# A four-layer attention kernel on one core: single V buffers, 64-row input and output groups, 77 resident weight pieces, first rows copied by VectorE and a new issue list

## The chip, the core and the metric

The kernel runs on one core of one Trainium2 chip. The metric is device time in microseconds (us), lower is better. Each time below is the median of several executions. The runs came in four sets, each on one chip with the kernel before beside it; since the kernel before takes 3261 to 3275 us in different sets, kernels of different sets are compared by their ratios to it.

## The reference

Two layers, A and B, are applied in the order A, B, A, B to x, 2048 rows of 640, each as x + layer(layernorm(x)). Layer A works through segments of 32 rows, one after the other, because each hands 8 memory rows to the next:

```python
for s in range(n_seg):                       # 64 segments
    h = concatenate([mem, xs], axis=1)       # 8 memory rows + 32 rows
    q, k, v = h @ Wq, h @ Wk, h @ Wv         # 32 heads of 192
    p = softmax(where(mask, q k^T * scale, -1e9))
    o = (p v) @ Wo
    mem = o[:, :M, :]                        # to the next segment
    outs.append(o[:, M:, :])
# layer B: 32 heads of 20; each row sees itself and 7 earlier rows, 2 apart; then @ wo
```

The weights of A are 31.5 MB in bf16 and do not all fit into the core's memory.

## The kernel before

The two A layers are run as two *lanes* of one step: lane 0 is segment t of the first A, lane 1 is segment t-2 of the second, so one weight load serves 80 columns. There are 66 steps with layer A; steps 0 and 1 and steps 64 and 65 have one lane, the 62 between have both. Layer B of the step before is woven into each step, and a 67th step holds B alone.

The weights of A are 128 pieces of 224 or 256 KB. `N_RES` of them stay in memory; the rest are loaded again in every step, through a ring of 8 buffers, as TensorE frees them.

```python
RING = 8
N_RES = 74
...
    def load_piece(self, u):
        ...
        if res:
            t_ = self.wres.tile([P, w], BF16, name="w_{}{}_{}{}".format(*u))
        else:
            t_ = self.wring.tile([P, P * PIECE[0]], BF16, name="w_ring")
        ...
        self.nc.sync.dma_start(out=t_[:, 0:w], in_=src)
```

Each step issues its parts in the order of a fixed list. `K3`, `Q3`, `V3` are projections of the third quad of heads (30 matmuls each), `KE3`, `QE3`, `VE3` their evictions from PSUM, `S` the scores, `T`/`TE` the transposes of V and their copy, `PO` the product with V, `R` the reciprocals of the softmax sums, `OT` the normalised outputs, `Oa`/`Ob` halves of the output projection. Names with small letters belong to layer B: `bo` transposes its outputs, `boE` evicts them, `by` is its output projection. The program gives every engine its own instructions in this order.

```python
ORDER = """
K0 V0 K0y KE0 Q0 QE0 VE0 K1 bst bmv KE1 Q1 S0 T0 E0 ...
... PO6 Oa3 T7 bo TE7 Ob3 R6 boE S7 OT16 E7 by OT26 ... X1 BSQ
""".split()
...
    def x_load(self, g):                       # 128 rows, one buffer
        self.xt[g] = self.xp.tile([P, NC, P], BF16, name="XT4")
        self.nc.scalar.dma_start(out=..., in_=self.x[g])
    def x_take(self, t):
        o = SEG * (t % 4)
        self.nc.gpsimd.tensor_copy(out=self.xin[t % 2][:, :, 0:SEG], in_=self.xt[t // 4][:, :, o:o + SEG])
...
            if n == "QE0":                     # in step t, nt = t + 1
                ...
                if nt % 4 == 3 and nt + 1 < self.n_seg:
                    self.x_load((nt + 1) // 4)
        if t == 0:
            self.load_b_weights()
```

Of the kernel before, what the change touches and what calls it, by code (L numbers as in the profile page):

```python
# [13 lines left out]
ALU = mybir.AluOpType  # L14
# [25 lines left out]
N_RES = 74  # L40
# [4 lines left out]
K0 V0 K0y KE0 Q0 QE0 VE0 K1 bst bmv KE1 Q1 S0 T0 E0 QE1 EM0 TE0 V1 br bap VE1 S1 K2 E1 Q2 T1 TE1 PO0 QE2 V2  # L45
KE2 R0 EM1 VE2 V3 bq S2 OT10 VE3 bqE E2 T2 OT20 T3 PO1 TE2 TE3 K3 R1 bk qx1 bkE qx0 KE3 OT11 V4 Q3 VE4 bs3
OT21 EM2 bs1 be3 PO2 QE3 bv be1 bs0 bvE Q4 be0 S3 Oa0 K4 eb0 qx2 R2 bs2 Oa1 QE4 OT12 E3 EM3 bs5 KE4 Q5 OT22
be2 S4 be5 QE5 PO3 Ob0 E4 T4 R3 K5 V5 EM4 KE5 bs4 VE5 eb5 eb2 TE4 OT13 V6 be4 OT23 eb3 eb1 VE6 S5 PO4 T5 Ob1
E5 Oa2 TE5 EM5 bt eb4 K6 btE R4 OT14 Q6 KE6 OT24 QE6 bp1 T6 PO5 on1 Ob2 R5 TE6 S6 E6 K7 V7 KE7 bp0 OT15 OT25
EM6 on0 Q7 QE7 VE7 PO6 Oa3 T7 bo TE7 Ob3 R6 boE S7 OT16 E7 by OT26 EM7 Oa5 byE LSQ PO7 Oa4 lst LMV R7 Ob4 Oa6  # L50
OT17 Ob5 OT27 Ob6 O7x LR O7y LAP O7z MEMa MEMb X1 BSQ
# [52 lines left out]
class Kernel:  # L104
    def __init__(self, ctx, tc, xT, m0T, wA, wqkv, wo, out):
# [7 lines left out]
        self.n_seg = 4 * xT.shape[0]  # L113
# [13 lines left out]
        self.n_big = self.n_ot = 0  # L127
        self.build_consts()

    def build_consts(self):  # L130
# [9 lines left out]
        def pers(name, shape, n, dt=BF16, zero=True):  # L140
            ts = []
            for j in range(n):
                t_ = cp.tile(shape, dt, name=f"{name}{j}")
                if zero:
                    nc.vector.memset(t_[:], 0.0)
                ts.append(t_)
            return ts
# [3 lines left out]
        self.m0T = pers("m0T", [P, NC, NM], 1, zero=False)[0]  # L151
        self.KF = pers("KF", [P, 4 * NT + 48], 2)
        self.Kz = pers("Kz", [P, 4 * NT + 48], 2)
        self.Vt = pers("Vt", [P, 1024], 2)
        for vt in self.Vt:
            for c in (192, 320, 704, 832):
                nc.vector.memset(vt[:, c:c + 64], 1.0)
        self.VT = pers("VT", [P, 6 * NT + 48], 2)
        self.x1 = pers("x1", [P, NC, NX], 1)[0]
        self.h2T = pers("h2T", [P, NC, NX], 1)[0]  # L160
        self.KB = pers("KB", [P, NBC, P], 1)[0]
        self.VB = pers("VB", [P, BH // 2, 2 * BD + 2], 1)[0]
        self.VTB = pers("VTB", [P, NC, P], 1)[0]
        nc.vector.memset(self.VB[:, :, BD:BD + 1], 1.0)
        self.On = pers("On", [P, 3 * P], 1)[0]
        self.eb = pers("EB", [P, BH // 2, 2, NX], 1, zero=False)[0]
        self.YT = pers("YT", [P, NC, P], 1, zero=False)[0]
        self.wqkv = cp.tile([P, NC, 3 * D], BF16, name="wqkv_sb")
# [47 lines left out]
        self.hmask = hm  # L216

    def load_b_weights(self):
        nc = self.nc
        nc.sync.dma_start(out=self.wqkv[:].rearrange("p c n -> p (c n)"), in_=self.b_src[0])  # L220
        nc.sync.dma_start(out=self.wo[:].rearrange("p m n -> p (m n)"), in_=self.b_src[1])
# [83 lines left out]
    def vE(self, i):  # L305
        vt = self.VT[i % 2][:, 0:6 * NT].rearrange("p (a n) -> p a n", a=6)
        self.nc.scalar.copy(out=vt[:, :, self.cs], in_=self.vp[i][:, 0:6 * NT].rearrange("p (a n) -> p a n", a=6)[:, :, self.cs])  # L307

    def a_t(self, i):
        nc = self.nc  # L310
        ps = self.big("ps_vt", (P, 6, P), BF16)
        for n in range(6):
            nc.tensor.transpose(out=ps[:, n, :], in_=self.VT[i % 2][:, NT * n:NT * n + P], identity=self.ident[:])  # L313
        self.tp[i] = ps

    def tE(self, i):
        nc = self.nc
        src = self.tp[i][0:NT].rearrange("p n e -> p (n e)").rearrange("p (a e) -> p a e", a=2)
        dst = self.Vt[i % 2][0:NT].rearrange("p (a e) -> p a e", a=2)
# [39 lines left out]
    def a_pv(self, i):  # L359
        nc = self.nc  # L360
        em = self.em[i]
        vt = self.Vt[i % 2]
# [8 lines left out]
    def ot1(self, i):  # L371
        self.n_ot += 1
        cs = self.cs
        ot = self.ap1.tile([P, 2, 3, NT], BF16, name="OT", tag=f"OT{self.n_ot % 3}")
# [95 lines left out]
    def b_proj(self, b, col0, name):  # L470
# [3 lines left out]
        for n in range(NBC):  # L474
            for c in range(NC):
                e0 = col0 + BHC * BD * n
# [335 lines left out]
```

## Time and profile before

| | before |
|---|---|
| median time | 3258.68 us (6 runs, 3249.38 to 3263.43) |
| TensorE busy | 96% |
| first weight matmul | 22.7 us |
| step 1 begins, step 2 begins | 97.4 us, 152.5 us |
| a two-lane step, mean of steps 4 to 62 | 48.30 us |
| step 64 begins; from there to the last matmul | 3147.1 us; 107.8 us |

A step begins at its first matmul of `K0`; these times are read from the trace. From the page, the engines (busy us, share of the span, instructions) and the DMA queues (packets, MB, share of 16 engines):

```profile
PE 3136.6 (96%) x85668; PEld 3083.6 (95%) x85668; DVE 2039.3 (63%) x6890; ACT 1993.5 (61%) x5215; POOL 40.8 (1%) x150
...
q1 hardware_dynamic: 524160, 901.84, 85.9%
q8 instruction: 671, 10.99, 1.3%
```

TensorE bounds the kernel. Queue q1 carries the weights; its packets took 86% of the time of the 16 DMA engines. Queue q8 brings TensorE's own instructions: 671 packets of 16 KiB, one for every 256 instructions.

The view by stretches, over 2700 us of the middle (busy us and number of instructions by engine, clock, DMA share, GB/s). A two-lane step has 1298 matmuls, so the count of matmuls in a fixed stretch is the rate: 2700 x 1298 / 72509 = 48.33 us a step.

```profile
core 0: us, PE busy (x) PEld busy (x) DVE busy (x) ACT busy (x) POOL busy (x), PEclk, DMA share, GB/s
300.00:3000.00 2700.00, 2662.75 (x72509) 2628.81 (x72506) 1739.79 (x5807) 1715.38 (x4419) 20.19 (x55) 1.00 0.88 282
```

30 matmuls of 80 columns take 1.08 us, 36 ns each. This agrees with columns / 2.4 GHz + 2.5 ns, which the Trainium skill states ("TensorE: Matmul & The Clock Gate", section Wait — 56ns, not 53.3ns?). Adding up a step's matmuls at such a pace gives 47.18 us. The missing 1.1 us are short gaps. The view of waits over the same stretch (engine, tile, line, releaser: us in all, times, longest):

```profile
PE ps_q L267 <- issue: 6.8, 14, 1.2
PE ps_k L267 <- issue: 5.5, 10, 1.0
PE ps_v L267 <- issue: 4.9, 8, 1.1
PE ps_s L335 <- issue: 2.9, 6, 0.7
...
PEld L594 <- issue: 10.7, 51, 0.5
```

The last line is one steady gap, 51 times in some 56 steps: the output projection of layer B (line 594) waits for `boE` on ScalarE. The others have no releaser, and their places change from step to step. One of them in the timeline (start, us, instruction, idle time before it):

```profile
642.63 0.38 PE L267 MATMUL ps_k<-hT_88,w_k_10_683 128*128 128x80 bf16 x6
643.99 0.23 PE L267 MATMUL ps_k<-hT_88,w_k_10_683 128*128 128x80 bf16 x2 [0.97 <-issue]
```

It stands within one resident piece, so it waits for no weight. In the trace, a packet of q8 had landed 1.58 us before 643.99 us, when the matmuls resumed. Besides the steady one at line 594, steps 4 to 62 hold 82 gaps over 0.15 us; 76 of them end 0.9 to 1.8 us after such a landing, three quarters 1.3 to 1.6 us after it. I call these 76 *fetch gaps*. Their size below is the excess of a start-to-start time over the matmul's pace, where it is over 0.15 us and ends 0.9 to 1.8 us after a landing, over steps 4 to 62. Before it is 0.75 us a step, and the gap at line 594 is 0.26 us.

A count in the trace shows what these gaps are. If all of TensorE's instructions (weight loads, matmuls, semaphore instructions) are numbered in order, 73 of the 76 stand in the same stretch of seven instructions of a block of 256; I call that place the *border*. A block with such a gap I call *late*; steps 4 to 62 hold 600 blocks. A border passes every 4.6 us. The next packet starts after it (1.53 us in the median), and TensorE resumes about 1.35 us after a late landing, so a packet that lands within some 3.2 us of the border (4.6 less 1.35, an estimate) should be in time for the next one. The trace bears it out: of 490 packets that landed within 3.2 us none left a late block, of 110 that landed later 73 did.

The start, in the timeline:

```profile
19.13 0.32 POOL L615 COPY xin_84<-XT_353 128x160 bf16<-128x160 bf16 x1
19.50 0.43 PE L429 MATMUL ps_st<-xin_84,ones 128*128 128x64 bf16 x5 [19.50 <-POOL xin_84 L615]
...
22.68 0.43 PE L267 MATMUL ps_k<-hT_88,w_k_00_387 128*128 128x40 bf16 x8 [2.39 <-DVE hT_88 L455]
```

GpSimd copies the first rows only after 18 us of building masks. And the largest wait of step 1, from the view of waits between 97 and 156 us:

```profile
PE ps_k L267 <- DMA w_ring<-in_wA_dram: 7.7, 1, 7.7
```

The ring's pieces stand behind the 3.28 MB of layer B's weights.

### The profile page before, as it was taken

The page shows a single profiled execution, that of the slowest core. Times are in us where ns is not written, and L with a number is a line of the kernel's source. Part 1 is how long each engine was busy: PE and PEld are TensorE (multiplying, and loading weights), DVE is VectorE, ACT ScalarE, POOL GpSimd, SP SyncE. Part 2 cuts the span into 40 slices and gives each one's busy share as a digit, 9 for nine tenths or more (in the row PEclk, how much of TensorE's full clock was granted, in tenths as well). Part 3 has the DMA queues.
Part 4 walks back from the last instruction along what each step waited for, and adds up shares of the span by engine and source line. Part 5 has one row for each costly group of instructions (what it writes and reads, how often), then busy time and mean ns, then how long its engine had stood idle before and what let it go on. Part 6 is the DMA issues. An engine that isn't in the chain of part 4 may idle for free.

```text
span 3258.3 us, 192948 instructions
## 1 busy us (share of the span) xinstructions
PE 3136.6 (96%) x85668; PEld 3083.6 (95%) x85668; DVE 2039.3 (63%) x6890; ACT 1993.5 (61%) x5215; POOL 40.8 (1%) x150
## 2 busy tenths in 40 slices
PE   5799999999999999999999999999999999999997
PEld 4799999999999999999999999999999999999996
DVE  2466666666666666666666666666666666666665
ACT  2366666566666666666666666666666666666654
POOL 2000000000000000000000000000000000000000
PEclk7799999999999999999999999999999999999999
DMA  9988988888888888888888888888888888888886
GB/s 325 324 279 279 291 277 284 282 277 283 279 281 284 281 283 281 280 280 282 278 289 277 275 291 276 283 287 279 284 279 279 288 280 288 277 282 279 286 286 215
DMA packets 529747, 919.44 MB, mean 282 GB/s; under 512 B 58896, under 2 KB 279184, under 8 KB 528784
## 3 DMA queue, kind: packets, MB, share of 16 engines
q1 hardware_dynamic: 524160, 901.84, 85.9%
q8 instruction: 671, 10.99, 1.3%
q10 hardware_dynamic: 4752, 5.26, 0.5%
q14 instruction: 164, 1.34, 0.1%
HBM read 904.24 MB, written 2.62 MB: 278 GB/s over the span
## 4 chain that ended last, share of the span: by engine, by line
PE 91%; ACT 3%; DMA 3%; issue 2%; POOL 0%; DVE 0%; ACTq 0%; POOLq 0%; SPq 0%
PE ps_k L267 17%; PE ps_v L267 17%; PE ps_q L267 17%; PE ps_vt L313 5%; PE ps_o L367 5%; PE ps_s L335 2%; PE ps_s L334 2%; PE ps_bq L477 2%; PE ps_by L594 2%; PE ps_bk L477 2%; PE ps_bs L530 2%; DMA w_ring<-in_wA_dram 2%; ACT R L354 2%; PE ps_bv L495 1%; PE ps_st L429 1%
## 5 line engine op out<-in xcount | busy, mean ns | idle before, releaser
L267 PEld LDWEIGHTS <-w_ring 128*128 128x128 bf16 x19866 | 881.1, 100 | 40.9 <-DMA w_ring<-in_wA_dram 19.7
L354 ACT ACTIVATE R<-ps_o 64x320 f32<-64x320 f32 (+1 forms) x1056 | 449.2, 425 | 357.1 <-PE ps_o L367 238.8
L302 DVE CAST QT<-ps_q 128x480 bf16<-128x480 f32 (+1 forms) x528 | 337.9, 640 | 426.9 <-PE ps_q L267 426.7
L296 ACT CAST KF_93<-ps_k 128x320 bf16<-128x320 f32 (+1 forms) x264 | 110.4, 418 | 424.5 <-PE ps_k L267 424.4
L387 PEld LDWEIGHTS <-w_ring 128*128 128x128 bf16 x6996 | 310.4, 100 | 13.1 <-issue 6.2
L322 DVE COPY Vt_103<-ps_vt 80x128 bf16<-80x128 bf16 x528 | 91.9, 213 | 307.4 <-PE ps_vt L313 307.0
L341 ACT ACTIVATE Em<-ps_s 80x320 bf16<-80x320 f32 (+1 forms) x528 | 224.8, 426 | 95.7 <-PE ps_s L335 92.0
L375 DVE TENSOR_TENSOR OT<-ps_o,R 128x320 bf16<-128x320 f32 (+1 forms) x528 | 251.8, 477 | 39.8 <-ACT R L356 18.1
L356 ACT ACTIVATE R<-R 128x320 f32<-128x320 f32 (+1 forms) x528 | 244.0, 462 | 16.8
L267 PE MATMUL ps_v<-hT_88,w_ring 128*128 128x80 bf16 (+1 forms) x3993 | 230.0, 201 | 5.2 <-DMA w_ring<-in_wA_dram 3.1
L267 PE MATMUL ps_v<-hT_90,w_ring 128*128 128x80 bf16 (+1 forms) x3993 | 228.8, 201 | 5.4 <-issue 4.7
L307 ACT CAST VT_115<-ps_v 128x480 bf16<-128x480 f32 (+1 forms) x264 | 144.4, 547 | 78.6 <-PE ps_v L267 78.1
L542 ACT ACTIVATE EB_130<-ps_bs 128x384 bf16<-128x384 f32 (+2 forms) x462 | 170.6, 415 | 33.7 <-PE ps_bs L530 32.1
L267 PE MATMUL ps_k<-hT_90,w_ring 128*128 128x80 bf16 (+1 forms) x3036 | 173.6, 201 | 12.2 <-DMA w_ring<-in_wA_dram 9.3
L347 DVE TENSOR_TENSOR Em<-Em,maskA 80x320 bf16<-80x320 bf16 (+1 forms) x528 | 165.2, 313 | 20.0 <-ACT Em L341 1.6
L267 PE MATMUL ps_k<-hT_88,w_ring 128*128 128x80 bf16 (+1 forms) x3036 | 173.5, 201 | 1.7 <-DMA w_ring<-in_wA_dram 1.2
L267 PE MATMUL ps_q<-hT_88,w_ring 128*128 128x80 bf16 (+1 forms) x2904 | 169.1, 201 | 3.3 <-issue 1.7
L381 DVE TENSOR_TENSOR OT<-ps_o,R 64x160 bf16<-64x160 f32 (+1 forms) x528 | 164.9, 312 | 7.2
L267 PE MATMUL ps_q<-hT_90,w_ring 128*128 128x80 bf16 (+1 forms) x2904 | 168.0, 201 | 0.0
L307 ACT CAST VT_113<-ps_v 128x480 bf16<-128x480 f32 (+1 forms) x264 | 144.4, 547 | 34.9 <-PE ps_v L267 29.6
L296 ACT CAST KF_95<-ps_k 128x320 bf16<-128x320 f32 (+1 forms) x264 | 110.7, 419 | 78.7 <-PE ps_k L267 77.9
L380 DVE TENSOR_TENSOR OT<-ps_o,R 64x160 bf16<-64x160 f32 (+1 forms) x528 | 158.5, 300 | 0.0
(3045 smaller groups left out, 8864.5 us busy)
## 6 DMA issues: line engine op xcount, KB each, us to landing
w_ring<-in_wA_dram SPq DMA_DIRECT2D x1914, 256.0 KB, 4.3
w_ring<-in_wA_dram SPq DMA_DIRECT2D x1650, 224.0 KB, 4.0
out_dram<-YT_131 ACTq DMA_DIRECT2D x16, 160.0 KB, 5.0
wqkv_sb<-in_wqkv_dram SPq DMA_DIRECT2D x1, 2400.0 KB, 10.1
wo_sb<-in_wo_dram SPq DMA_DIRECT2D x1, 800.0 KB, 11.5
w_k_00_387<-in_wA_dram SPq DMA_DIRECT2D x1, 256.0 KB, 3.0
w_k_10_406<-in_wA_dram SPq DMA_DIRECT2D x1, 256.0 KB, 3.9
w_v_10_439<-in_wA_dram SPq DMA_DIRECT2D x1, 256.0 KB, 4.3
```

Of the source, the lines that this page charges most:

```text
L267: self.nc.tensor.matmul(ps[:, NT * n + c0:NT * n + c1], lhsT=self.block(kind, i, h, k), rhs=hT[:, NT * c + c0:NT * c + c1], start=(h == 0 ...
L296: nc.scalar.copy(out=kf[:, :, :, cs], in_=pv[:, :, 0:3:2, cs])
L302: self.nc.vector.tensor_copy(out=qt[:, :, self.cs], in_=self.qp[i][:, 0:6 * NT].rearrange("p (a n) -> p a n", a=6)[:, :, self.cs])
L307: self.nc.scalar.copy(out=vt[:, :, self.cs], in_=self.vp[i][:, 0:6 * NT].rearrange("p (a n) -> p a n", a=6)[:, :, self.cs])
L341: self.nc.scalar.activation(out=e[0:NT, :, cs], in_=self.sv[i][0:NT, :, cs], func=ACT.Exp, scale=float(DH) ** -0.5)
L347: self.nc.vector.tensor_tensor(out=em[0:NT, :, cs], in0=em[0:NT, :, cs], in1=self.maskA[0:NT, cs].unsqueeze(1).to_broadcast([NT, 4, w]), o ...
L354: self.nc.scalar.activation(out=r[rows, :, :, self.cs], in_=d, func=ACT.Ln)
L356: self.nc.scalar.activation(out=rf, in_=rf, func=ACT.Exp, scale=-1.0)
L375: self.nc.vector.tensor_tensor(out=ot[:, :, 0:3:2, cs], in0=self.ov[:, :, 0:4:3, cs], in1=self.r[i][:, :, :, cs], op=ALU.mult)
L381: nc.vector.tensor_tensor(out=ot[64:P, :, 1, cs], in0=ov[0:64, :, 2, cs], in1=r[0:64, :, 1, cs], op=ALU.mult)
L387: self.nc.tensor.matmul(self.acc[c // 3][:, o:o + self.cs.stop - self.cs.start], lhsT=self.block("o", i, h, k), rhs=ot[:, m, self.cs], sta ...
L542: self.nc.scalar.activation(out=self.eb[:, h:h + n, a, :], in_=self.bsp[c][:, NX * o:NX * (o + n)].rearrange("p (h n) -> p h n", h=n), fun ...
```

## The change

Its intent is to free memory (one V buffer instead of two, input and output in groups of 64 rows), to use it for three more resident pieces and a fourth buffer for inputs of the output projection, to start sooner, to load layer B's weights in four parts during step 1, and to arrange the issue list so that the single buffers cost nothing. The core of the diff:

```diff
-N_RES = 74
+N_RES = 77
 ORDER = """
-K0 V0 K0y KE0 Q0 QE0 VE0 K1 bst bmv KE1 Q1 S0 T0 E0 QE1 EM0 TE0 V1 br bap VE1 S1 K2 E1 Q2 T1 TE1 PO0 QE2 V2
... (7 lines)
+K0 Q0 K0y V0 KE0 Q1 QE0 S0 VE0 K1 QE1 E0 bst KE1 T0 V1 EM0 TE0 bmv Q2 VE1 PO0 br S1 QE2 bap R0 K2 T1 E1 V2 KE2
... (4 lines)
+bs5 eb3 be5 Oa1 S6 PO5 eb5 VE6 E6 Ob1 eb4 bt eb1 T6 EM6 btE R5 V7 TE6 OT15 OT25 bp0 bp1 K7 on0 VE7 PO6 Q7 T7
+KE7 on1 Oa2 bo Ob2 R6 QE7 TE7 S7 boE by OT16 E7 OT26 Oa5 EM7 byE Oa3 PO7 Oa4 LSQ lst Ob3 Oa6 Ob4 R7 LMV OT17
... (1 line)
+LAST = """ ...                      # the list for the step that holds layer B alone
-        self.Vt = pers("Vt", [P, 1024], 2)
-        self.VT = pers("VT", [P, 6 * NT + 48], 2)
+        self.Vt = pers("Vt", [P, 1024], 1)[0]
+        self.VT = pers("VT", [P, 6 * NT + 48], 1)[0]
-        ot = self.ap1.tile([P, 2, 3, NT], BF16, name="OT", tag=f"OT{self.n_ot % 3}")
+        ot = self.ap1.tile([P, 2, 3, NT], BF16, name="OT", tag=f"OT{i % 4}")
...
+    def first_rows(self):                    # called before most buffers are cleared
...
+        nc.vector.tensor_copy(out=self.xin[0][:, :, 0:SEG], in_=self.xt[0][:, :, 0:SEG])
+        for n in ("LSQ", "lst", "LMV", "LR", "LAP"):
+            self.l_piece(n, 0)
...
-        self.xt[g] = self.xp.tile([P, NC, P], BF16, name="XT4")
+        self.xt[g] = self.xp.tile([P, NC, NX], BF16, name="XT2")
...
+            if t == 1 and n in ("bst", "bap", "bqE", "bvE"):
+                self.load_b_weights(("bst", "bap", "bqE", "bvE").index(n))
...
-                if nt % 4 == 3 and nt + 1 < self.n_seg:
-                    self.x_load((nt + 1) // 4)
-        if t == 0:
-            self.load_b_weights()
+                if nt % 2 == 1 and nt + 1 < self.n_seg:
+                    self.x_load((nt + 1) // 2)
```

Left out: the clearing of layer B's buffers moves from VectorE to GpSimd, layer B's weights are laid out in three parts, and the last group of heads has its own mask.

More of the change, by code (lines that the diff above doesn't have):

```diff
@@ L44 @@
 ORDER = """
-K0 V0 K0y KE0 Q0 QE0 VE0 K1 bst bmv KE1 Q1 S0 T0 E0 QE1 EM0 TE0 V1 br bap VE1 S1 K2 E1 Q2 T1 TE1 PO0 QE2 V2
-KE2 R0 EM1 VE2 V3 bq S2 OT10 VE3 bqE E2 T2 OT20 T3 PO1 TE2 TE3 K3 R1 bk qx1 bkE qx0 KE3 OT11 V4 Q3 VE4 bs3
-OT21 EM2 bs1 be3 PO2 QE3 bv be1 bs0 bvE Q4 be0 S3 Oa0 K4 eb0 qx2 R2 bs2 Oa1 QE4 OT12 E3 EM3 bs5 KE4 Q5 OT22
-be2 S4 be5 QE5 PO3 Ob0 E4 T4 R3 K5 V5 EM4 KE5 bs4 VE5 eb5 eb2 TE4 OT13 V6 be4 OT23 eb3 eb1 VE6 S5 PO4 T5 Ob1
-E5 Oa2 TE5 EM5 bt eb4 K6 btE R4 OT14 Q6 KE6 OT24 QE6 bp1 T6 PO5 on1 Ob2 R5 TE6 S6 E6 K7 V7 KE7 bp0 OT15 OT25
-EM6 on0 Q7 QE7 VE7 PO6 Oa3 T7 bo TE7 Ob3 R6 boE S7 OT16 E7 by OT26 EM7 Oa5 byE LSQ PO7 Oa4 lst LMV R7 Ob4 Oa6
-OT17 Ob5 OT27 Ob6 O7x LR O7y LAP O7z MEMa MEMb X1 BSQ
+K0 Q0 K0y V0 KE0 Q1 QE0 S0 VE0 K1 QE1 E0 bst KE1 T0 V1 EM0 TE0 bmv Q2 VE1 PO0 br S1 QE2 bap R0 K2 T1 E1 V2 KE2
+TE1 EM1 VE2 bq OT10 Q3 OT20 bqE S2 PO1 E2 QE3 T2 R1 V3 K3 VE3 TE2 KE3 V4 qx0 T3 OT11 bk OT21 EM2 VE4 PO2 TE3
+S3 bkE E3 Q4 bs0 K4 EM3 R2 be0 QE4 bs1 K5 OT12 Q5 be1 OT22 KE4 PO3 T4 KE5 qx2 qx1 S4 R3 Oa0 E4 QE5 V5 bs2 TE4
+OT13 VE5 EM4 K6 be2 S5 Q6 OT23 eb0 KE6 QE6 PO4 T5 bs3 Ob0 TE5 eb2 E5 bv EM5 R4 bs4 be3 OT14 V6 be4 OT24 bvE
+bs5 eb3 be5 Oa1 S6 PO5 eb5 VE6 E6 Ob1 eb4 bt eb1 T6 EM6 btE R5 V7 TE6 OT15 OT25 bp0 bp1 K7 on0 VE7 PO6 Q7 T7
+KE7 on1 Oa2 bo Ob2 R6 QE7 TE7 S7 boE by OT16 E7 OT26 Oa5 EM7 byE Oa3 PO7 Oa4 LSQ lst Ob3 Oa6 Ob4 R7 LMV OT17
+Ob6 Ob5 OT27 O7x O7y LR LAP O7z MEMa MEMb X1 BSQ
+""".split()
+LAST = """
+bst bmv br bap bq bqE bk qx0 bkE qx1 bs0 be0 bs1 be1 qx2 bv bs2 be2 eb0 bs3 be3 eb1 bvE bs4 be4 eb2 bs5 be5 eb3
+bt eb4 btE eb5 bp0 on0 bp1 on1 bo boE by byE
 """.split()
@@ L112, in __init__ @@
         self.out = out
-        self.n_seg = 4 * xT.shape[0]
+        self.n_seg = 2 * xT.shape[0]
         pool = lambda name, bufs, **kw: ctx.enter_context(tc.tile_pool(name=name, bufs=bufs, **kw))
@@ L126, in __init__ @@
         self.cur = {}
-        self.n_big = self.n_ot = 0
+        self.n_big = 0
+        self.xt, self.ots, self.qxs, self.kp, self.qp, self.vp, self.tp = {}, {}, {}, {}, {}, {}, {}
+        self.x_load(0)
         self.build_consts()
@@ L138, in build_consts, with pers @@
         self.ones = ones
-        def pers(name, shape, n, dt=BF16, zero=True):
+        def pers(name, shape, n, dt=BF16, zero=True, eng=nc.vector):
             ts = []
@@ L144, in pers @@
                 if zero:
-                    nc.vector.memset(t_[:], 0.0)
+                    eng.memset(t_[:], 0.0)
                 ts.append(t_)
@@ L151, in build_consts @@
         self.m0T = pers("m0T", [P, NC, NM], 1, zero=False)[0]
+        self.first_rows()
         self.KF = pers("KF", [P, 4 * NT + 48], 2)
         self.Kz = pers("Kz", [P, 4 * NT + 48], 2)
-        self.Vt = pers("Vt", [P, 1024], 2)
-        for vt in self.Vt:
-            for c in (192, 320, 704, 832):
-                nc.vector.memset(vt[:, c:c + 64], 1.0)
-        self.VT = pers("VT", [P, 6 * NT + 48], 2)
-        self.x1 = pers("x1", [P, NC, NX], 1)[0]
-        self.h2T = pers("h2T", [P, NC, NX], 1)[0]
-        self.KB = pers("KB", [P, NBC, P], 1)[0]
-        self.VB = pers("VB", [P, BH // 2, 2 * BD + 2], 1)[0]
-        self.VTB = pers("VTB", [P, NC, P], 1)[0]
-        nc.vector.memset(self.VB[:, :, BD:BD + 1], 1.0)
-        self.On = pers("On", [P, 3 * P], 1)[0]
+        self.Vt = pers("Vt", [P, 1024], 1)[0]
+        for c in (192, 320, 704, 832):
+            nc.vector.memset(self.Vt[:, c:c + 64], 1.0)
+        self.VT = pers("VT", [P, 6 * NT + 48], 1)[0]
         self.eb = pers("EB", [P, BH // 2, 2, NX], 1, zero=False)[0]
-        self.YT = pers("YT", [P, NC, P], 1, zero=False)[0]
-        self.wqkv = cp.tile([P, NC, 3 * D], BF16, name="wqkv_sb")
+        self.YT = pers("YT", [P, NC, NX], 1, zero=False)[0]
+        self.wqkv = cp.tile([P, 3, NC, D], BF16, name="wqkv_sb")
         self.wo = cp.tile([P, NC, D], BF16, name="wo_sb")
@@ L216, in build_consts, with load_b_weights @@
         self.hmask = hm
-    def load_b_weights(self):
+        nl = BH % BHC
+        hl = cp.tile([P, nl, NX], BF16, name="hmask_last")
+        nc.gpsimd.memset(hl[:], 1.0)
+        nc.gpsimd.affine_select(out=hl[:], in_=hl[:], compare_op=ALU.is_ge, fill=0.0, base=BD * nl - P,
+                                pattern=[[-BD, nl], [0, NX]], channel_multiplier=1)
+        nc.gpsimd.affine_select(out=hl[:], in_=hl[:], compare_op=ALU.is_ge, fill=0.0, base=BD - 1 - BD * nl + P,
+                                pattern=[[BD, nl], [0, NX]], channel_multiplier=-1)
+        self.hmask_last = hl
+        self.x1 = pers("x1", [P, NC, NX], 1, eng=nc.gpsimd)[0]
+        self.h2T = pers("h2T", [P, NC, NX], 1, eng=nc.gpsimd)[0]
+        self.KB = pers("KB", [P, NBC, P], 1, eng=nc.gpsimd)[0]
+        self.VB = pers("VB", [P, BH // 2, 2 * BD + 2], 1, eng=nc.gpsimd)[0]
+        self.VTB = pers("VTB", [P, NC, P], 1, eng=nc.gpsimd)[0]
+        nc.gpsimd.memset(self.VB[:, :, BD:BD + 1], 1.0)
+        self.On = pers("On", [P, 3 * P], 1, eng=nc.gpsimd)[0]
+    def load_b_weights(self, part):
         nc = self.nc
-        nc.sync.dma_start(out=self.wqkv[:].rearrange("p c n -> p (c n)"), in_=self.b_src[0])
-        nc.sync.dma_start(out=self.wo[:].rearrange("p m n -> p (m n)"), in_=self.b_src[1])
+        if part == 3:
+            nc.sync.dma_start(out=self.wo[:].rearrange("p m n -> p (m n)"), in_=self.b_src[1])
+        else:
+            nc.sync.dma_start(out=self.wqkv[:, part].rearrange("p c n -> p (c n)"), in_=self.b_src[0][part])
     def block(self, kind, i, h, k):
@@ L305, in vE @@
     def vE(self, i):
-        vt = self.VT[i % 2][:, 0:6 * NT].rearrange("p (a n) -> p a n", a=6)
+        vt = self.VT[:, 0:6 * NT].rearrange("p (a n) -> p a n", a=6)
         self.nc.scalar.copy(out=vt[:, :, self.cs], in_=self.vp[i][:, 0:6 * NT].rearrange("p (a n) -> p a n", a=6)[:, :, self.cs])
@@ L312, in a_t @@
         for n in range(6):
-            nc.tensor.transpose(out=ps[:, n, :], in_=self.VT[i % 2][:, NT * n:NT * n + P], identity=self.ident[:])
+            nc.tensor.transpose(out=ps[:, n, :], in_=self.VT[:, NT * n:NT * n + P], identity=self.ident[:])
         self.tp[i] = ps
@@ L318, in tE @@
         src = self.tp[i][0:NT].rearrange("p n e -> p (n e)").rearrange("p (a e) -> p a e", a=2)
-        dst = self.Vt[i % 2][0:NT].rearrange("p (a e) -> p a e", a=2)
+        dst = self.Vt[0:NT].rearrange("p (a e) -> p a e", a=2)
         two = lambda v, c, step, w: v[:, :, c:c + 2 * step].rearrange("p a (j e) -> p a j e", j=2)[:, :, :, 0:w]
@@ L361, in a_pv @@
         em = self.em[i]
-        vt = self.Vt[i % 2]
+        vt = self.Vt
         ps = self.ps_one.tile([P, 2, 512], F32, name="ps_o", tag="o")
@@ L371, in ot1 @@
     def ot1(self, i):
-        self.n_ot += 1
         cs = self.cs
-        ot = self.ap1.tile([P, 2, 3, NT], BF16, name="OT", tag=f"OT{self.n_ot % 3}")
+        ot = self.ap1.tile([P, 2, 3, NT], BF16, name="OT", tag=f"OT{i % 4}")
         self.nc.vector.tensor_tensor(out=ot[:, :, 0:3:2, cs], in0=self.ov[:, :, 0:4:3, cs], in1=self.r[i][:, :, :, cs], op=ALU.mult)
@@ L468, in b_ln_apply, with b_proj @@
         self.ln_big(self.x1, self.bmr, self.h2T[:].rearrange("p c (l n) -> p c l n", l=2))
-    def b_proj(self, b, col0, name):
+    def b_proj(self, part, name):
         nc = self.nc
@@ L475, in b_proj @@
             for c in range(NC):
-                e0 = col0 + BHC * BD * n
-                nc.tensor.matmul(ps[:, NX * n:NX * (n + 1)], lhsT=self.wqkv[:, c, e0:e0 + P], rhs=h[:, c, :],
+                e0 = min(BHC * BD * n, D - P)
+                nc.tensor.matmul(ps[:, NX * n:NX * (n + 1)], lhsT=self.wqkv[:, part].rearrange("p c n -> p (c n)")[:, D * c + e0:D * c + e0 + P], rhs=h[:, c, :],
                                  start=(c == 0), stop=(c == NC - 1))
@@ L493, in b_v @@
             for c in range(NC):
-                e0 = 2 * D + P * n
-                nc.tensor.matmul(ps[:, NX * n:NX * (n + 1)], lhsT=self.wqkv[:, c, e0:e0 + P], rhs=self.h2T[:, c, :],
+                e0 = P * n
+                nc.tensor.matmul(ps[:, NX * n:NX * (n + 1)], lhsT=self.wqkv[:, 2, c, e0:e0 + P], rhs=self.h2T[:, c, :],
                                  start=(c == 0), stop=(c == NC - 1))
@@ L522, in b_qexp @@
             nc.vector.tensor_tensor(out=qx[:, c % 2, 0:nh, :], in0=self.qb[:, c, :].unsqueeze(1).to_broadcast([P, nh, NX]),
-                                    in1=self.hmask[:, 0:nh, :], op=ALU.mult)
+                                    in1=self.hmask[:] if nh == BHC else self.hmask_last[:], op=ALU.mult)
         self.qxs[g] = qx
@@ L605, in b_yE @@
         if 0 <= seg1 < self.n_seg:
-            o = SEG * (seg1 % 4)
+            o = SEG * (seg1 % 2)
             nc.vector.tensor_tensor(out=self.YT[:, :, o:o + SEG], in0=pv[:, :, SEG:NX], in1=x1[:, :, SEG:NX], op=ALU.add)
     def x_load(self, g):
-        self.xt[g] = self.xp.tile([P, NC, P], BF16, name="XT4")
+        self.xt[g] = self.xp.tile([P, NC, NX], BF16, name="XT2")
         self.nc.scalar.dma_start(out=self.xt[g][:].rearrange("p c n -> p (c n)"), in_=self.x[g])
     def x_take(self, t):
-        o = SEG * (t % 4)
-        self.nc.gpsimd.tensor_copy(out=self.xin[t % 2][:, :, 0:SEG], in_=self.xt[t // 4][:, :, o:o + SEG])
+        o = SEG * (t % 2)
+        self.nc.gpsimd.tensor_copy(out=self.xin[t % 2][:, :, 0:SEG], in_=self.xt[t // 2][:, :, o:o + SEG])
     def y_store(self, g):
@@ L624, in prologue @@
         nc = self.nc
-        self.xt, self.ots, self.qxs, self.kp, self.qp, self.vp, self.tp = {}, {}, {}, {}, {}, {}, {}
         self.qt, self.em, self.r, self.bsp, self.bpv, self.sv = {}, {}, {}, {}, {}, {}
         self.acc = None
-        self.x_load(0)
+    def first_rows(self):
+        nc = self.nc
         nc.scalar.dma_start(out=self.m0T[:].rearrange("p c n -> p (c n)"), in_=self.mem0)
-        self.x_take(0)
-        nc.vector.tensor_copy(out=self.lanes(self.hT[0][:, 0:NC * NT])[:, :, 0, 0:NM], in_=self.m0T[:])
+        nc.vector.tensor_copy(out=self.xin[0][:, :, 0:SEG], in_=self.xt[0][:, :, 0:SEG])
         for n in ("LSQ", "lst", "LMV", "LR", "LAP"):
             self.l_piece(n, 0)
+        nc.vector.tensor_copy(out=self.lanes(self.hT[0][:, 0:NC * NT])[:, :, 0, 0:NM], in_=self.m0T[:])
     def l_piece(self, n, nt):
@@ L658, in b_piece @@
         elif n == "bq":
-            self.bqp = self.b_proj(b, 0, "ps_bq")
+            self.bqp = self.b_proj(0, "ps_bq")
         elif n == "bqE":
@@ L662, in b_piece @@
         elif n == "bk":
-            self.bkp = self.b_proj(b, D, "ps_bk")
+            self.bkp = self.b_proj(1, "ps_bk")
         elif n == "bkE":
@@ L729, in step @@
             self.x_take(nt)
-        for n in ORDER:
+        for n in ORDER if a else LAST:
             if n[0] in "Ll":
@@ L741, in step @@
                 self.b_piece(n, b)
+            if t == 1 and n in ("bst", "bap", "bqE", "bvE"):
+                self.load_b_weights(("bst", "bap", "bqE", "bvE").index(n))
             if n == "QE0":
                 yseg = t - 2 - LAG
-                if yseg >= 0 and yseg % 4 == 3:
-                    self.y_store(yseg // 4)
-                if nt % 4 == 3 and nt + 1 < self.n_seg:
-                    self.x_load((nt + 1) // 4)
-        if t == 0:
-            self.load_b_weights()
+                if yseg >= 0 and yseg % 2 == 1:
+                    self.y_store(yseg // 2)
+                if nt % 2 == 1 and nt + 1 < self.n_seg:
+                    self.x_load((nt + 1) // 2)
     def run(self, ctx):
@@ L755, in run @@
                 self.step(t)
-            self.y_store((self.n_seg - 1) // 4)
+            self.y_store((self.n_seg - 1) // 2)
 @with_exitstack
@@ L773, in laid_out @@
     x = A_x[0]
-    xT = x.reshape(x.shape[0] // P, P, D).transpose(0, 2, 1)
+    xT = x.reshape(x.shape[0] // NX, NX, D).transpose(0, 2, 1)
     w = {k: a.reshape(D, NQUAD, QE).transpose(1, 0, 2) for k, a in (("k", A_Wk), ("q", A_Wq), ("v", A_Wv))}
@@ L785, in laid_out @@
     wo = np.stack([wo[0, 0:P], wo[1, 192:], wo[0, P:256], wo[1, 64:192], np.concatenate([wo[0, 256:], wo[1, 0:64]])], 1).reshape(P, -1)
-    out = {"xT": chunks(xT), "m0T": chunks(A_mem0[0].T[None])[0], "wA": wA, "wqkv": chunks(B_wqkv[None])[0], "wo": wo}
+    out = {"xT": chunks(xT), "m0T": chunks(A_mem0[0].T[None])[0], "wA": wA, "wqkv": chunks(B_wqkv.reshape(D, 3, D).transpose(1, 0, 2)), "wo": wo}
     return {k: np.ascontiguousarray(v) for k, v in out.items()}
@@ L804 @@
     (_, S, _), dt = _OUTS[0]
-    groups = S // P
-    args.append(nc.dram_tensor("out_0_dram", (groups, P, NC * P), _mybir.dt.from_np(np.dtype(dt)), kind="ExternalOutput").ap())
+    groups = S // NX
+    args.append(nc.dram_tensor("out_0_dram", (groups, P, NC * NX), _mybir.dt.from_np(np.dtype(dt)), kind="ExternalOutput").ap())
     with _tile.TileContext(nc) as tc:
@@ L809 @@
     r = _run(nc, [arrays], core_ids=[0])
-    got = r.results[0]["out_0_dram"].reshape(groups, P, NC, P)
+    got = r.results[0]["out_0_dram"].reshape(groups, P, NC, NX)
     return np.ascontiguousarray(got.transpose(0, 3, 2, 1)).reshape(1, S, D)
```

## The prediction

> **What bounds it now.** TensorE: 96% busy, and the chain of waits puts 91% of the span on it. In the timeline a two-lane step takes 48.3 us on average (47.5 to 49.5). 30 matmuls of 80 columns take 1.08 us, 36 ns each; the Trainium skill ("TensorE: Matmul & The Clock Gate", Wait — 56ns, not 53.3ns?) states columns / 2.4 GHz + 2.5 ns, which is the same. Adding a step's matmuls at this pace gives about 47.2 us, 1.1 us less:
> - about 0.26 us: layer B's output projection waits for a ScalarE eviction, in nearly every step.
> - about 0.75 us: gaps of 0.2 to 1.4 us with releaser "issue", at places that drift. Most end 1.3 to 1.6 us after a 16 KiB packet of the DMA queue of kind "instruction" has landed (671 packets, one per 256 TensorE instructions). "Runtime: NRT & Kernel Launch", Instruction fetch mechanics, calls block fetches mostly hidden; here they are not. Such a packet starts later when more weight pieces are in flight (0.9 us at one to two pieces, 1.9 us at four to five).
>
> Elsewhere: the first weight matmul starts at 22.6 us: the first rows' copy stands behind 18 us of masks on GpSimd; the weight queue stands still from 12.8 to 23.4 us. Step 0 is bound by loading all 128 pieces (0.66 us each) and ends at 97.3 us. Step 1 then stands 7.85 us behind layer B's 3.28 MB of weights and takes 55.1 us. The two last layer-A steps have one lane but take 47 us, since fetches arrive only every 4.6 us. The last step, a chain of latencies, takes 20 us.
>
> **What the change does.**
> 1. First rows taken by VectorE, without the masks ahead. First matmul at about 7.5 us, no stop of the weight stream: step 0 ends at 2.8 + 128 x 0.66 = about 88 us. Gain 9 us.
> 2. Layer B's weights come in four parts during step 1, which has spare DMA: step 1 takes about 48 us. Gain 7 us.
> 3. 77 resident pieces: 51 streamed a step instead of 54, 5.6% fewer bytes (901.8 to about 853 MB). The stream bounds no steady step; I expect only the fetch gaps to fall from 0.75 to about 0.6 us a step: 9 us.
> 4. New issue list. TensorE's work is unchanged. Along the new list, with the trace's durations, I find no steady wait left, also none from the single V buffers: each eviction of V follows the transposes of the V before, each copy of transposed V the product before. The 0.26 us wait and small ones go: 0.3 us a step, 19 us.
> 5. Last step in its own order, smaller last store; fetch-bound one-lane steps slightly quicker: 4 us.
>
> Sum 48 us, all on the chain: about **3210 us**, 8 in 10 between 3188 and 3234. Faster by over 2%: 0.18; within 2%: 0.81; slower: 0.01.
>
> **Right or wrong, in the profile.** First weight matmul near 7.5 us; step 1 starts near 88, step 2 near 136 us; steady steps mean 47.85 us; no gap before the output projection; "issue" gaps fewer; weight queue near 853 MB; one-lane steps near 46 us.
>
> **What would make it wrong.** Fetch gaps may nearly vanish with less weight traffic (3180), or, since TensorE asks for instructions sooner once waits are gone, stay and take back part of point 4 (3225). Single V buffers could add waits.

## The result, and the profile after

| | before | after |
|---|---|---|
| median time | 3261.29 us (20 runs) | 3216.29 us (10 runs, 3205.45 to 3219.59) |
| ratio | | 0.9858, 95% interval 0.9846 to 0.9871 |
| first weight matmul | 22.7 us | 7.4 us |
| step 1 begins, step 2 begins | 97.4, 152.5 us | 99.0, 148.9 us |
| a two-lane step, mean of steps 4 to 62 | 48.30 us | 47.66 us |
| fetch gaps; gap before `by`, a step | 0.75; 0.26 us | 0.40; 0 us |
| step 64 begins; from there to the last matmul | 3147.1; 107.8 us | 3105.5; 106.3 us |

A ratio is the mean time of one kernel's fast runs over that of the other's of the same rounds, so it is not quite the ratio of the medians quoted. The other rows are from the two profiled executions. Between them, 43.1 us were won up to the last matmul: 3.6 until step 2 begins, 38.0 in the 62 two-lane steps, 1.4 after them.

The same lines of the page after:

```profile
PE 3126.3 (97%) x85668; PEld 3082.3 (96%) x85668; DVE 2061.5 (64%) x6878; ACT 2012.2 (63%) x5215; POOL 43.0 (1%) x159
...
q1 hardware_dynamic: 496368, 854.97, 83.3%
q8 instruction: 671, 10.99, 1.4%
```

TensorE has as many instructions as before; 47 MB of weights are gone. The stretch of 2700 us:

```profile
300.00:3000.00 2700.00, 2684.77 (x73542) 2660.68 (x73539) 1787.68 (x5898) 1756.77 (x4484) 19.70 (x56) 1.00 0.86 270
```

This is 47.65 us a step. The waits in it:

```profile
PE ps_q L285 <- issue: 5.7, 11, 1.1
PE ps_v L285 <- issue: 2.2, 6, 0.6
PE ps_s L353 <- issue: 2.0, 3, 1.0
PE ps_k L285 <- issue: 1.3, 3, 0.5
```

The four lines sum to 11.2 us, against 20.1 us for the four of before, and there is no line for layer B's output projection (now line 611) any more. In step 1, between 97 and 150 us, where a wait of 7.7 us for a ring piece stood, the largest line for one is now:

```profile
PE ps_k L285 <- DMA w_ring<-in_wA_dram: 1.6, 2, 1.2
```

The start is where the profile is not as hoped. The timeline:

```profile
4.06 0.21 DVE L648 COPY xin_86<-XT_79 128x160 bf16<-128x160 bf16 x1 [1.89 <-DMA XT_79<-in_xT_dram]
...
7.42 0.43 PE L285 MATMUL ps_k<-hT_90,w_k_00_383 128*128 128x40 bf16 x8 [2.30 <-DVE hT_90 L472]
...
25.31 0.32 POOL L632 COPY xin_88<-XT_79 128x160 bf16<-128x160 bf16 x1
25.66 0.33 ACTq L628 DMA_DIRECT2D XT_543<-in_xT_dram  x1
26.09 0.36 ACT L325 CAST VT_137<-ps_v 128x240 bf16<-128x240 f32 x1 [15.40 <-POOL xin_88 L632]
...
26.50 0.82 PE L331 MATMUL ps_vt<-ident,VT_137 128*128 128x128 bf16 x6 [8.57 <-ACT VT_137 L325]
```

The first matmul comes 15 us sooner, but TensorE then stands for 8.6 us. With groups of 64 rows the second input load falls into step 0. It stands in ScalarE's queue ahead of the first eviction of V, and it may overwrite the one input buffer only after GpSimd has copied segment 1's rows out of it, at 25.3 us, behind its masks. In the kernel before, the first such load came in step 2. While TensorE stands, no ring buffer is freed, and the weight queue stands too.

### The profile page after: what moved, and what is told of

Its sections match the earlier page's. It is cut to its first block, busy times and chain, and to the rows that moved or that the text cites. A ratio compares the mean times of both kernels' runs of the same rounds, so it can differ in the third digit from the quotient of the medians.

```text
span 3214.9 us, 192749 instructions
## 1 busy us (share of the span) xinstructions
PE 3126.3 (97%) x85668; PEld 3082.3 (96%) x85668; DVE 2061.5 (64%) x6878; ACT 2012.2 (63%) x5215; POOL 43.0 (1%) x159
## 3 DMA queue, kind: packets, MB, share of 16 engines
q1 hardware_dynamic: 496368, 854.97, 83.3%
q14 instruction: 164, 1.34, 0.1%
## 4 chain that ended last, share of the span: by engine, by line
PE 95%; DMA 3%; issue 1%; POOL 1%; DVE 0%; ACT 0%; SPq 0%; POOLq 0%; ACTq 0%; DVEq 0%
PE ps_k L285 17%; PE ps_q L285 17%; PE ps_v L285 17%; PE ps_vt L331 5%; PE ps_o L385 5%; PE ps_s L353 2%; PE ps_s L352 2%; PE ps_bq L494 2%; PE ps_bk L494 2%; PE ps_bs L547 2%; DMA w_ring<-in_wA_dram 2%; PE ps_by L611 2%; PE ps_bv L512 2%; PE ps_st L446 1%; PE ps_bo L575 1%
## 5 line engine op out<-in xcount | busy, mean ns | idle before, releaser
L285 PEld LDWEIGHTS <-w_ring 128*128 128x128 bf16 x19008 | 839.4, 100 | 24.0 <-DMA w_ring<-in_wA_dram 13.8
L340 DVE COPY Vt_131<-ps_vt 80x128 bf16<-80x128 bf16 x1056 | 184.4, 214 | 246.0 <-PE ps_o L385 132.3
L404 PEld LDWEIGHTS <-w_ring 128*128 128x128 bf16 x6402 | 284.7, 100 | 7.8 <-DMA w_ring<-in_wA_dram 2.9
L331 PE MATMUL ps_vt<-ident,VT_137 128*128 128x128 bf16 x3168 | 268.0, 221 | 9.3 <-ACT VT_137 L325 8.6
L385 PE MATMUL ps_o<-Em,Vt_131 80*128 80x80 bf16 (+1 forms) x4224 | 237.9, 199 | 0.8 <-DVE QT L320 0.8
L342 DVE COPY Vt_131<-ps_vt 80x512 bf16<-80x512 bf16 x528 | 215.8, 409 | 0.9 <-PE ps_s L353 0.9
L285 PE MATMUL ps_q<-hT_90,w_ring 128*128 128x80 bf16 (+1 forms) x3498 | 201.0, 201 | 3.8 <-DMA w_ring<-in_wA_dram 2.6
L331 PEld LDWEIGHTS <-VT_137 128*128 128x128 bf16 x3168 | 192.7, 99 | 9.9 <-ACT VT_137 L325 8.7
L285 PE MATMUL ps_q<-hT_92,w_ring 128*128 128x80 bf16 (+1 forms) x3498 | 200.3, 201 | 0.3 <-DMA w_ring<-in_wA_dram 0.3
L385 PEld LDWEIGHTS <-Vt_131 80*128 80x128 bf16 x4224 | 184.0, 98 | 1.0 <-DVE QT L320 0.9
L285 PE MATMUL ps_v<-hT_92,w_ring 128*128 128x80 bf16 (+1 forms) x3036 | 173.1, 201 | 2.4 <-DMA w_ring<-in_wA_dram 1.5
L285 PE MATMUL ps_k<-hT_90,w_ring 128*128 128x80 bf16 (+1 forms) x2970 | 171.3, 201 | 3.3 <-DMA w_ring<-in_wA_dram 1.9
(3210 smaller groups left out, 8476.1 us busy)
```

The costliest lines, as they stand in the source:

```text
L285: self.nc.tensor.matmul(ps[:, NT * n + c0:NT * n + c1], lhsT=self.block(kind, i, h, k), rhs=hT[:, NT * c + c0:NT * c + c1], start=(h == 0 ...
L331: nc.tensor.transpose(out=ps[:, n, :], in_=self.VT[:, NT * n:NT * n + P], identity=self.ident[:])
L342: nc.vector.tensor_copy(out=dst[:, :, 0:4:3, :], in_=src[:, :, 0:3:2, :])
L385: nc.tensor.matmul(ov[:, pr, b, self.cs], lhsT=vt[0:NT, 512 * pr + P * b:512 * pr + P * (b + 1)], rhs=em[0:NT, 2 * pr + b // 2, self.cs], ...
L404: self.nc.tensor.matmul(self.acc[c // 3][:, o:o + self.cs.stop - self.cs.start], lhsT=self.block("o", i, h, k), rhs=ot[:, m, self.cs], sta ...
```

## The experiments

Twelve runs in three sets. "Two-lane step" and "fetch gaps" are from the profiled execution of each, over steps 4 to 62; single profiles of the changed kernel gave 0.40, 0.40 and 0.63 us of fetch gaps in three sets, so differences of 0.2 us between sets mean little. The profiled execution need not be a typical one: the profile with 0.63 us is of the slowest run of its four (3236.23 us, median 3225.63).

### One: an early second take

```diff
         nc.vector.tensor_copy(out=self.xin[0][:, :, 0:SEG], in_=self.xt[0][:, :, 0:SEG])
+        nc.vector.tensor_copy(out=self.xin[1][:, :, 0:SEG], in_=self.xt[0][:, :, SEG:NX])
...
-        if nt < self.n_seg:
+        if 1 < nt < self.n_seg:
             self.x_take(nt)
```

> The changed kernel, but VectorE also takes the second lane-0 rows (segment 1) right after the first, so that GpSimd's copy behind its masks is no longer in the way of the second input group's load, which stands in ScalarE's queue before its first eviction of V. Theory A: the 8.6 us wait of TensorE on that eviction goes, the weight queue no longer stops, step 1 starts near 89 us instead of 98.8, and the whole gains about 9 us (near 3207 us). Rival: step 0 is bound by the load of 128 pieces whatever stands in between; then step 1 starts within 3 us of 98.8 and the time stays within 4 us of the changed kernel's 3216.

Measured: 3218.18 us, ratio to before 0.9852 (0.9833 to 0.9870). The wait is gone and step 1 begins at 91.8 us. So the start answers to theory A, but the time is what the rival expected. The changed kernel was not in this set. It was therefore run again, with more rounds and the changed kernel beside it:

> The early second take once more, with more rounds and beside the changed kernel on the same chip. If what step 0 gains (7 us in the first profile) is kept, it is 5 to 9 us faster than the changed kernel; if it is given back later, within 2 us.

> The changed kernel beside the run before it, on the same chip: 0.986 of the kernel before, within 0.2%.

Measured in this set: with the early take 3222.10 us, ratio 0.9834 (0.9813 to 0.9855); the changed kernel 3225.63 us, ratio 0.9852 (0.9827 to 0.9877). The timeline of the early take:

```profile
9.81 0.37 ACTq L628 DMA_DIRECT2D XT<-in_xT_dram  x1
```

The load is issued at 9.8 us instead of 25.7. In the profiles step 1 begins at 89.4 us against 101.0, and step 2 at 141.2 against 153.2. So the 8.6 us wait did cause the lost start, and the rival (step 0 bound by the load of 128 pieces alone) falls as far as the start goes. The whole is 3.5 us faster by the medians, below the 5 to 9 us expected; the two intervals overlap, and in the first set this kernel's ratio was 0.9852, that of the changed kernel here. It has the lowest ratio of the correct versions, but its lead over the changed kernel is not clear of noise, and whether the start's gain is kept to the end is not shown.

### Two: which part made the two-lane steps faster

Three kernels, each one step from the next: 74 resident pieces in the changed kernel; two V buffers besides; the old issue list besides (the last step keeps its new list).

```diff
-N_RES = 77
+N_RES = 74
```

> The changed kernel with 74 resident pieces as before. Theory T (traffic): instruction fetches come late because of weight pieces in flight, so the gaps with releaser issue go from about 0.40 us a two-lane step back towards 0.75, the two-lane steps from 47.66 to about 47.95 us, the time to about 3235 us. Rival L (list): the new list itself made the gaps rarer; the steps stay within 0.1 us of 47.66 and the time within 6 us of 3217.

```diff
-        self.Vt = pers("Vt", [P, 1024], 1)[0]
-        self.VT = pers("VT", [P, 6 * NT + 48], 1)[0]
+        self.Vt = pers("Vt", [P, 1024], 2)
+        self.VT = pers("VT", [P, 6 * NT + 48], 2)
...   (and [i % 2] wherever they are used; 74 pieces)
```

> As the run with 74 resident pieces, with two V buffers each again. Theory: the single buffers cost nothing, since the list orders every write after the last read; the time is within 4 us of the run with 74 pieces and single buffers. Rival: the single buffers cost hidden waits, and this is faster by over 6 us.

```diff
 ORDER = """
-K0 Q0 K0y V0 KE0 Q1 QE0 S0 VE0 K1 ...
+K0 V0 K0y KE0 Q0 QE0 VE0 K1 bst bmv ...   (the whole list of before)
```

> As the run with 74 pieces and two V buffers, with the old issue list for all but the last step. Theory T: the list is worth the removed wait before the output projection of layer B and small waits, 0.3 to 0.35 us a two-lane step, so this is about 20 us slower than the run with the new list (near 3255 us), with two-lane steps near 48.3 us. Rival L: the list is worth the fall of the issue gaps too, 0.6 us a step, about 40 us slower than the run before it (that is, the run before it stays near 3217).

Measured:

| | time | ratio to before, 95% interval | two-lane step | fetch gaps |
|---|---|---|---|---|
| 74 pieces | 3254.34 us | 0.9968 (0.9944 to 0.9993) | 48.15 us | 0.85 us |
| and two V buffers | 3261.58 us | 0.9977 (0.9962 to 0.9992) | 48.31 us | 1.00 us |
| and the old list | 3278.08 us | 1.0031 (1.0015 to 1.0047) | 48.60 us | 1.04 us |

*The list.* It is worth 16.5 us (3278.08 less 3261.58). Views of waits, middle 2700 us, with the old list and then with the new one, for the weight loads of layer B's output projection (line 612 in both):

```profile
PEld L612 <- issue: 9.7, 49, 0.2
```

```profile
PEld L612 <- issue: 0.2, 1, 0.2
```

The gap goes and the fetch gaps hardly move (1.04 to 1.00 us; 116 and 114 late blocks of 600). So the list removed a wait, as theory T says; it did not make late fetches rarer, and rival L falls.

*Single V buffers.* No cost shows: the run with single buffers is not slower than the run with two (0.9968 and 0.9977, overlapping). By the medians it is 7.2 us faster, more than the 4 us allowed for, but with the sign against the rival.

*Three resident pieces.* From 74 to 77 the ratio goes from 0.9968 to 0.9858, 0.9866 and 0.9852 in the three sets with the changed kernel, 0.9859 on average: 1.1%, 36 us. This was expected at about 18 (3235 less 3217). The stretch of 2700 us with 74 pieces:

```profile
300.00:3000.00 2700.00, 2670.12 (x72839) 2639.15 (x72837) 1771.18 (x5839) 1736.24 (x4437) 19.70 (x56) 1.00 0.90 284
```

It is 48.11 us a step, 0.46 us more than with 77 pieces: 28 us over 62 steps. This profile is of the fastest of its four runs (3249.00 us).

*What stays open.* The run with the old list, 74 pieces and two V buffers differs from the kernel before only in small things and the start, which won it nothing, yet it is 0.31% slower. One suspect was tried alone, 64-row groups in the kernel before:

```diff
-        self.n_seg = 4 * xT.shape[0]
+        self.n_seg = 2 * xT.shape[0]
...   (input and output in groups of NX = 64 rows, as in the change; nothing else)
```

> The kernel before with 64-row input and output groups alone. The run with the old list, 74 pieces and two V buffers was 0.3% slower than the kernel before, though only small things differ. If the small groups cost it (twice the input and output DMAs among the weights), this is 0.2 to 0.5% slower than before, by more issue gaps; if not, it is within 0.1%, and the loss lies elsewhere (placement of tiles, the loads of layer B).

Measured: 3266.17 us against 3261.35, ratio 1.0016 (0.9983 to 1.0049). That is undecided. Some 10 us are lost by a part of the change that these runs do not name. The profiles show where they go: the fetch gaps are 0.75 us a step in the kernel before, 0.86 with 64-row groups alone and 1.04 in the run with the old list. What makes the fetches later there stays open.

### Three: are the gaps really late fetches, and how do they depend on traffic

First the changed kernel once more, as company on this chip, and then the same kernel without its weight stream:

> The changed kernel itself, so that the other runs of this set stand beside it on one chip: within 0.3% of 0.986 of the kernel before; fetch gaps near 0.4 us a two-lane step.

```diff
     def load_piece(self, u):
         q = u[3]
         w = P * PIECE[q]
+        if self.t >= 2:
+            return self.last[q]        # whatever the ring held last: wrong on purpose
...   (self.t is the step, self.last the last streamed piece of each size)
```

> The changed kernel, but from step 2 on no piece is streamed: the 51 streamed pieces read whatever the ring held last, so the result is wrong on purpose. TensorE's instructions are the same, only the weight traffic is gone. Theory T (late instruction fetches come from weight traffic): the issue gaps all but vanish, two-lane steps take 47.2 to 47.25 us, and the two one-lane steps fall from 45 to under 42 us, as a fetch then takes less than 4.6 us; about 3180 us in all. Rival S (the sequencer's own fetch is too slow for this instruction stream, traffic or not): gaps stay over 0.25 us a step and one-lane steps stay near 45 us.

Measured: the changed kernel 3215.08 us, ratio 0.9866 (0.9838 to 0.9893), fetch gaps 0.40 us. Without the stream 3173.24 us, ratio 0.9735 (two runs of it; wrong, relative error 0.022). The stretch:

```profile
300.00:3000.00 2700.00, 2700.00 (x74198) 2681.47 (x74195) 1803.49 (x5945) 1769.91 (x4519) 20.15 (x57) 1.00 0.02 6
```

TensorE is busy 2700.00 of 2700 us, a step takes 47.23 us, and the view of waits for TensorE is empty there. The same matmuls and weight loads, fetched the same way (670 packets of q8 against 671), cause no gap once the weights stay out of the DMA engines: a packet now starts 0.16 us after the border in the median, against 1.25 us in the changed kernel. Rival S falls. The one-lane steps show the same thing. Stretches over step 64, before, after and without the stream:

```profile
3147.00:3194.00 47.00, 38.63 (x1307) 37.35 (x1304) 25.88 (x105) 22.75 (x79) 0.00 (x0) 0.96 0.88 287
```

```profile
3105.00:3150.00 45.00, 37.52 (x1307) 36.22 (x1303) 26.36 (x105) 23.10 (x79) 0.00 (x0) 1.00 0.89 280
```

```profile
3079.00:3115.00 36.00, 35.63 (x1289) 35.10 (x1286) 25.60 (x102) 22.99 (x79) 0.00 (x0) 1.00 0.02 5
```

About 1300 matmuls take 47, 45 and 36 us. With one lane each matmul is short, TensorE runs through 256 instructions sooner than the next packet arrives, and the packet's arrival sets the pace: in step 64 of before packets start every 4.7 us on average, and seven gaps of 0.86 to 2.0 us follow their landings; without the stream they start every 3.7 us and TensorE is busy 35.63 of 36 us.

Then the dose: three pieces less and six pieces more than the changed kernel streams.

```diff
+        if self.t >= 2 and u in self.skip:                    # 3 of the 51, evenly spread
+            return next(v for r, v in self.units.items() if r[3] == q)
...   (self.skip is made at the start)
```

> The changed kernel, but from step 2 on three of the 51 streamed pieces, evenly spread, read a resident piece instead of being loaded (the result is wrong on purpose): the traffic that 80 resident pieces would leave. Gaps were 0.85, 0.40 and 0 us a two-lane step at 54, 51 and 0 pieces. Theory C (a fetch is late only where its delay exceeds the 4.65 us that TensorE takes for 256 instructions, so each piece less is worth less than the one before): gaps near 0.2 us, two-lane steps near 47.45 us, about 15 us faster than the changed kernel. Rival P (proportional to the pieces streamed): gaps near 0.37 us, time within 4 us of the changed kernel.

```diff
-N_RES = 77
+N_RES = 71
```

> The changed kernel with 71 resident pieces, 57 streamed a step. Theory C: gaps near 1.3 us a two-lane step, two-lane steps near 48.6 us, 60 to 75 us slower than the changed kernel. Rival P: 0.45 us, within 10 us of the changed kernel. If TensorE begins to wait for the ring's pieces themselves (releaser DMA), the stream has become a bound of its own.

Measured, with the kernels above; the pieces are those streamed in each step. Late blocks are of 600. The last column is the median time from a border to the start of the next packet:

| pieces streamed | time, ratio to before (95% interval) | two-lane step | fetch gaps | late blocks | packet starts after |
|---|---|---|---|---|---|
| 57 | 3307.32 us, 1.0102 (1.0075 to 1.0129) | 49.01 us | 1.65 us | 155 | 1.94 us |
| 54 | 3254.34 us, 0.9968 (0.9944 to 0.9993) | 48.15 us | 0.85 us | 108 | 1.76 us |
| 51 (changed kernel, three sets) | 3216.29, 3215.08, 3225.63 us, 0.9859 on average | 47.66, 47.66, 47.91 us | 0.40, 0.40, 0.63 us | 48, 44, 76 | 1.25, 1.32, 1.62 us |
| 48 | 3219.28 us, 0.9821 (0.9795 to 0.9847) | 47.59 us | 0.33 us | 39 | 1.32 us |
| 0 | 3173.24 us, 0.9735 (0.9696 to 0.9774) | 47.24 us | 0 us | 0 | 0.16 us |

A gap of a late block is about 0.5 us in each of these runs; it is the number of late blocks that changes.

The kernel with 48 pieces passed the comparison with the reference although three of its pieces are wrong; its result is not to be used. Stretches of 2700 us with 57 and with 48 pieces:

```profile
300.00:3000.00 2700.00, 2637.49 (x71585) 2597.48 (x71582) 1738.29 (x5729) 1706.43 (x4355) 19.36 (x55) 1.00 0.91 294
```

```profile
300.00:3000.00 2700.00, 2687.24 (x73619) 2663.62 (x73616) 1790.39 (x5902) 1758.46 (x4489) 19.68 (x56) 1.00 0.82 256
```

Going down by three pieces each time wins 1.34%, 1.09% and 0.38% of the time before, by the ratios, and the last 48 pieces together only 0.86%. So the pieces from 57 down to 51 are worth far more each than the rest, and rival P (proportional) falls, on the run with 57 pieces above all, which is 82 us slower than the changed kernel of its set where P allowed 10 and theory C 60 to 75. Whether the first three are worth more than the second three is within the noise. The run with 48 pieces alone would not decide it: it is 6.4 us faster by the medians, between the two forecasts, and its 0.33 us of fetch gaps are nearer to P's 0.37 than to C's 0.2. With 57 pieces TensorE also waits for the pieces themselves, though still less than for instructions (of the 1.65 us of fetch gaps, the late blocks make 1.4):

```profile
PE ps_k L285 <- issue: 9.6, 22, 0.9
PE ps_q L285 <- DMA w_ring<-in_wA_dram: 9.3, 17, 1.2
PE ps_q L285 <- issue: 8.6, 18, 1.0
PE ps_v L285 <- issue: 8.4, 19, 1.0
PE ps_acc L404 <- issue: 7.2, 15, 1.0
```

### Four: fewer ring buffers for one more piece

```diff
-RING = 8
-N_RES = 77
+RING = 6
+N_RES = 78
...   (and the early second take of experiment one)
```

> The kernel with the early second take, with 6 ring buffers instead of 8 and one more resident piece (78). Theory T: fewer pieces can be in flight and 2% fewer bytes go, so fetches start sooner: gaps under 0.35 us a two-lane step, 5 to 12 us faster than the changed kernel on this chip. Rival: six buffers hold 5.6 us of weights, too little for landings of 4 to 5 us, TensorE waits for pieces (releaser DMA of the ring), and it is 5 us or more slower.

Measured: 3223.19 us, ratio 0.9887 (0.9857 to 0.9918), against 3215.08 us for the changed kernel in the same set, which has no early take; the two intervals overlap. Fetches do start sooner, as the theory wants: a packet starts 0.97 us after the border in the median and only 6 blocks of 600 are late, against 1.32 us and 44 in the changed kernel of this set. But a two-lane step takes 47.83 us, and the largest waits of TensorE, over the whole span, are now for pieces:

```profile
PE ps_q L285 <- DMA w_ring<-in_wA_dram: 12.4, 26, 1.3
PE ps_v L285 <- DMA w_ring<-in_wA_dram: 11.3, 17, 2.5
PE ps_k L285 <- DMA w_ring<-in_wA_dram: 5.2, 14, 1.7
```

The gaps that end 0.9 to 1.8 us after a landing still sum to 0.48 us a step, but here nearly all of them stand elsewhere than at the border. The miss is useful: with six buffers the late fetches all but go, and waits for pieces take their place. The rival's mechanism is right; that the whole is slower is not clear of noise. Seven buffers were not tried.

## Why the prediction was right or wrong

The time was forecast at 3210 us and came at 3216.29 us, inside the range. The sum was nearly right because terms were wrong in opposite directions: points 1 and 2 brought 12 us less than forecast and some 10 us were lost without a name, while point 3 brought about 27 us more. That these cancelled is luck.

1. *The start, "Gain 9 us".* The first matmul came at 7.4 us as forecast, but step 1 began at 99.0 us, not at 88. The step that failed is "no stop of the weight stream". The input load in ScalarE's queue waited for GpSimd's masks, TensorE waited 8.6 us, and the ring stood. The two runs with an early take show it: step 1 then begins at 91.8 and 89.4 us. I had looked at who copies the first rows, not at what the smaller input groups put into ScalarE's queue.
2. *Layer B's weights, "Gain 7 us".* The 7.7 us wait is gone and step 1 took 50.0 us instead of 55.1, a little over the forecast 48. Points 1 and 2 together gave 3.6 us in the profiles instead of 16.
3. *Three more resident pieces.* The bytes were right (854.97 MB for 853), the mechanism too: no steady step was bound by the stream, only fetches came late, and without the stream the gaps vanish. The size was wrong: "from 0.75 to about 0.6 us a step: 9 us". Against before, the gaps fell to 0.40 us, 22 us over 62 steps; with the rest of the change held fixed, the three pieces are worth about 36 us by the ratios, 28 of them in fetch gaps (0.85 to 0.40 us a step). I had taken the mean delay of a fetch to fall a little and the gaps with it. The dose runs show a steep curve instead, and the traces why: a packet costs nothing if it lands within some 3.2 us of the border. With 74 pieces it landed after 2.85 us in the median and 108 blocks of 600 were late; with 77 it landed after 2.36 us and 48 were late. So near that edge a few per cent of traffic change how many fetches are late at all.
4. *The issue list, "19 us".* Right: 16.5 us in the run that puts the old list back, and it is the gap before layer B's output projection that went. "Also none from the single V buffers" is right as well.
5. *The last step and the one-lane steps, "4 us".* 1.4 us in the profiles. The part of layer B alone takes 15.6 us instead of 15.8 from its first statistics matmul to the last matmul; its own list won next to nothing. The one-lane steps stayed bound by fetches.

The prediction's doubt, that TensorE would ask for instructions sooner once waits are gone and so give back part of point 4, did not come true: with the old list and the new one the fetch gaps are alike. The unexplained 0.31% of the run with the old list hides in the sum; without it the gain would have been larger.

## What to carry to other kernels

A kernel whose main engine runs some hundred thousand short instructions may stream its program from memory too, as this one does, and here bulk loads made that stream late before they were a bound themselves: look for short gaps without a releaser that wander through the program, compare them with the landings of the instruction queue, and count whether they stand at one place of the block of 256. Where such fetches land close to the point at which they begin to cost, as here, a few per cent less traffic can be worth more than it looks, and the next few per cent less. And whenever a transfer moves earlier or becomes more frequent, ask what stands behind it in the issuing engine's queue and what its buffer still waits for.

## What the Trainium skill lacked or had wrong

- "Runtime: NRT & Kernel Launch", section Instruction fetch mechanics, calls the cost of crossing from one 16 KiB block to the next "mostly hidden". Here it is not: TensorE lost 0.75 us of each 48.3 us step before, 0.40 us after, 1.65 us with 57 streamed pieces, and some 8 us of a one-lane step (step 64 takes 45.1 us after, 36.7 us without the stream). The page has no word on bulk DMA traffic making fetches late.
- "DMA: Bandwidth & Descriptors", section Queues, rings and completion order, says that an engine takes turns between queues packet by packet. That fits with instruction packets starting later when more pieces are in flight (in the kernel before, 1.1 us after the border on average with three pieces issued and not landed, 2.35 us with seven; the prediction's figures are from another way of counting), but no page gives such a figure, and no run here isolates the turn-taking.
- No page says how to read a stretch without clock records. The view by stretches gives a granted clock of 0.50 in step 0 of the kernel before (60 to 100 us) and 1.00 in that of the changed kernel, but the trace of the changed kernel holds no clock record before 103.2 us. In step 0 of both, matmuls of 40 columns start 33 ns apart, against 25 ns in step 64. So the pace does not tell the two apart, and the 1.00 is not to be believed.
